# First batch by token halves, the inverse's updates on TensorE and ScalarE, and loads issued earlier, in a fused Nystrom attention and squared-ReLU kernel

## The chip, the cores and the metric

The kernel runs on one core of one Trainium2 chip. The metric is the device time of one execution in microseconds. The same program runs before and after on the same inputs.

## The reference

Eight batches of eight heads, 576 tokens, head size 64. The attention is approximated with 32 landmarks per head; the result goes through two GEMMs with a squared ReLU between them.

```python
B, H, S, D = q.shape                      # 8, 8, 576, 64
m = 32
q_lm = q.reshape(B, H, m, S // m, D).mean(axis=3)
k_lm = k.reshape(B, H, m, S // m, D).mean(axis=3)
A  = sm(q, k_lm)                          # softmax of a @ b.T / 8 over the last axis
Bm = sm(q_lm, k_lm)
C  = sm(q_lm, k)
Z = Bm.transpose(0, 1, 3, 2) / (norm1(Bm) * norminf(Bm) + 1e-06)
for _ in range(6):
    Z = 2 * Z - Z @ Bm @ Z
x = (A @ Z @ C @ v)                       # then heads side by side: 4608 x 512
h = x @ w_in                              # 512 -> 2048
r = np.maximum(h, 0.0)
out = (r * r) @ w_out                     # 2048 -> 512
```

## The kernel before

Each batch has three parts. `attention(b)` forms the landmark sums, the three softmaxes A, B and C, the inverse Z by six rounds, and `C @ v`; it then folds Z, `C @ v` and `w_in` together into a matrix G (256 x 2048, `g_mm`, L925 and L928), so that the first GEMM is A^T against G and x itself is never formed. `mlp_in(b)` has 16 steps f, one per 128 hidden columns: four matmuls of 288 tokens each (`in_mm`, L947) into two PSUM banks, a relu of all 576 tokens to bf16 (L964 on ScalarE, L966 on VectorE), and a square (L972 on ScalarE, L974 on VectorE or GpSimd). `mlp_out(b)` does the second GEMM by 128 tokens, 16 matmuls of 512 columns into one bank each (`o_mm`, L1019), evicts and stores; in batch 0 each tile is made in two runs of eight matmuls.

A is made in two parts, one per four heads (`a_mm` L872): transposed out of PSUM (`a_t` L883), its maximum (L887), the subtraction (L889), the exponential (L892), the sum, the reciprocal, the product (L900) and the transposition to A^T (`a_xp` L911). `in_mm` reads both parts, `("AT", z, 0)` and `("AT", z, 1)`.

In batch 0 the inverse is a chain. The state `st` holds P = Z B and Z side by side, 32 x 32 blocks of four heads on the partitions. A round is `nv_0` on TensorE (L688, eight matmuls of 32 x 32 blocks) and the update `upd` on VectorE (L703): the new state is 2 st minus the product. The sixth round gives `zt` (L713).

The loads go through GpSimd's queue: half of q or k of a batch (L372, 288 KB), a quarter of v (L377, 144 KB), a quarter of `w_in` (L404, 512 KB) or of `w_out` (L412, 512 KB). They are cast to bf16 on the way. Piece n of `w_in` is read by `g_mm` n, piece j of `w_out` by the `o_mm` of f = 4j to 4j + 3. GpSimd's other instructions stand in the same queue.

Nothing is scheduled at run time. `Plan.add` only records operations with what they read and write, and `Plan.emit` writes them out in the order of the list `ORDER`: each number holds an operation, its engine and its PSUM bank, and a negative one a run of dummy matmuls of zeros (`fill`, L453) that keep TensorE busy. Every engine then works through its own instructions in that order. A second table, `PACE`, adds waits: an operation in it does not begin before another operation is done, also where no data passes between them. Loads in particular are held back in this way: before, the first piece of `w_in` waits for `st0z`, the start of the inverse's state (L666).

Of the kernel before, what the change touches and what calls it, by code (L numbers as in the profile page):

```python
# [8 lines left out]
P = 128  # L9
# [22 lines left out]
SUMS = 2  # L32
LN_EXP_SET = 6
# [7 lines left out]
    592, 32, 344, 280, 72, 472, 720, -384, 2628, 2696, 2309, -56, 1606, 160, 200, 784, 408, 536, 1496, 1560, -56,  # L41
    1664, 1924, 1736, 1432, 2000, 2368, 1798, 1872, 2759, 2440, 2180, 2501, 2832, 3014, 3088, 2248, 3144, 3208, -16,
    6016, 6096, 2568, 2887, 2952, 1368, 2052, 920, 856, 984, 3280, 3344, 3408, 6160, 1048, 3472, 3536, 3600, 3664,
    2120, -34, 9733, 9800, 3728, 9158, 9216, 9288, 3780, 3920, 4992, 3856, 4738, 9349, 5072, 3972, 4048, 6598, 9416,
    5128, 4816, 5192, 1112, -37, 4100, 4176, -69, 4228, 4936, -13, 5381, 6232, 4872, -8, 5248, 6280, 6672, 4304, 5448,
    6736, 5520, 4356, 4432, 8454, 6352, 4487, 5320, 5632, 4560, 1176, 1240, 4615, 6416, 8900, 5584, 5712, 6808, 8512,
    1304, 4688, 5760, 6488, 5890, 6856, 6928, 6992, 6544, 7064, 9029, 9104, 9607, 8584, 8646, 5960, 5832, 7168, 7120,
    -42, 7362, 8968, 9680, 8712, 9860, 9936, 8773, 7960, 7304, 8024, 7240, -30, 15168, 15366, 8848, 8088, 18392,
    18328, 7440, 15440, 7496, 9992, 10056, 15240, 10128, 15304, 10192, 9476, 7554, 7696, 15552, 15750, 9552, 7624,
    8216, -13, 15938, 15504, 16132, 15624, 10256, 15816, 16008, 10384, 16320, 16514, 10448, 16710, 16200, 13252,  # L50
    15696, 10512, 16072, 15888, 16584, 656, 10328, 16400, -16, 7744, 10690, 16776, 7816, 13328, -19, 16902, 8152,
    17092, 10576, 10640, 10832, 18456, 10768, 16272, 10896, 7880, 16464, 16968, 13826, 17160, 16648, 17224, 8280,
    17280, 17352, 16840, 10950, 13904, 11024, 11088, -47, 12098, 20164, 13968, 11141, 18264, 8408, 22982, 11216,
    12176, 12232, 23040, 23104, 23168, 12296, 12352, 17032, 20224, 11280, 11333, 18759, 18816, 23232, 23296, 23360,
    13392, 25240, 12432, 18880, 18944, 19008, 19072, 23424, 11408, 12488, 11472, 14032, 11525, 24720, 12552, 11600,
    25296, 14088, 23496, 17474, 11664, 17544, 17664, 24784, 25360, 20288, 14160, 17736, 17800, 13464, 17416, 19136,
    12741, 12816, 12614, 14224, 12688, 8344, 20352, 12880, 20416, -10, 11717, 17856, 13512, 17608, 17928, 20480,
    11792, 11920, 21574, 21632, 21696, 11856, 11973, 25552, 12994, 20544, 12944, 25424, 24400, 12048, 24472, 19200,
    13072, 17992, 21760, 13125, 21824, 13192, 25624, 18048, 19272, 18120, 14786, 14920, 14856, 20608, 20680, 21888,
    21952, 14976, -53, 14402, 24536, 18648, 13584, -21, 14596, 22016, 18184, 26000, 24600, 13648, 25104, 22151, 22208,  # L60
    14296, 14352, 14480, 13720, 14536, 24856, 25688, 25752, 13776, 24920, 22272, 22336, 22400, 22464, 25496, 14664,
    24984, 14728, 25168, 22088, 22528, 24664, 31490, 31684, 25040, 25816, 23558, 23616, 15048, 22592, 18584, 25872,
    31560, 34648, 18520, 31752, 25936, 26050, 23680, 31876, 34776, 15112, 23744, 26128, 26192, 26312, 23808, 23872,
    22672, 23936, 22944, 26248, 26384, 24000, 26448, 26512, 26584, 28480, 28560, 28354, 31624, 28432, 34712, 19335,
    26640, 19392, 31944, 28624, 32008, 19456, 31816, 19520, 19584, 19648, 26948, 18712, 19712, 19776, 26704, 26768,
    26832, 20741, 20800, 26896, 27088, 27024, 20864, 20928, 20992, 21056, 21120, 19856, 20128, 20000, 28744, 28680,
    24080, 24224, 27160, 42136, 21184, 28808, 21264, 32066, 27204, 27280, 28872, 27344, 32256, 34584, 29200, 34904,
    30150, 30224, 20064, 19936, 32136, 29060, 32450, 32328, 32200, 27397, 27472, 27544, 32640, 30288, 29574, 29648,
    32520, 32712, 29128, 32408, 28933, 29000, 32834, 33024, 32912, 22880, 27588, 27664, 27728, 35078, 42640, 36423,
    36480, 33218, 27780, 21536, 33096, 42960, 43032, 32584, 27856, 27928, 35136, 33408, 29712, 32776, 36544, 29316,  # L70
    21472, 29784, 33488, 33288, 29264, 29392, 33602, 33792, 30360, 36608, 36672, 43344, 36736, 27972, 28048, 28112,
    32968, 33160, 33672, 28176, 33864, 29832, 33544, 35200, 35264, 42192, 42264, 42712, 33986, 42776, 42840, 29904,
    30408, 41816, 34176, 34248, 22816, 28228, 28304, 33352, 21408, 29968, 21344, 33736, 43096, 43160, 43224, 35328,
    35392, 36800, 36864, 36928, 35456, 35520, 29444, 29512, 34368, 34056, 34440, 34312, 36992, 30480, 42576, 37056,
    37120, 22752, 35584, 35648, 35712, 30544, 30616, 30914, 31048, 42512, 30720, 30792, 30992, 30864, 39108, 34504,
    34120, 39168, 42328, 30672, 33928, 39232, 37765, 37824, 35776, 39296, 31106, 31176, 31296, 31368, 31432, 37888,
    37952, 30040, 38016, 38080, 37184, 37248, 34968, 38144, 31248, 30096, 48898, 48968, 41872, 41936, 42896, 43280,
    42000, 35840, 35904, 24288, 35968, 42064, 39360, 45760, 42384, 42448, 43458, 43536, 43600, 43656, 43720, 24160,
    38208, 52184, 36032, 45840, 37312, 52440, 37376, 43792, 39424, 39488, 51992, 43856, 38272, 49032, 43920, 44048,
    37448, 45890, 45968, 44112, 46032, 46280, 46152, 39552, 39616, 37600, 38336, 38400, 46088, 39680, 44176, 44240,  # L80
    38464, 39744, 43408, 39808, 39872, 38528, 36112, 38592, 24352, 46216, 43992, 44359, 44496, 38656, 46608, 38720,
    38792, 39936, 44304, 40000, 52120, 49088, 46470, 49282, 49160, 37536, 40064, 52376, 40453, 49472, 46536, 35032,
    44432, 37664, 59024, 44568, 44614, 49360, 40512, 49666, 49224, 44688, 52056, 40576, 44752, 57872, 57936, 49544,
    49736, 40640, 44806, 36192, 46343, 46408, 46672, 44880, 44944, 47552, 46978, 47632, 40704, 44998, 45072, 34840,
    45144, 58008, 40768, 40832, 49800, 38944, 40136, 40896, 49856, 40960, 47696, 47768, 38880, 49608, 50054, 45188,
    47056, 47120, 49928, 41024, 41088, 50240, 58072, 49416, 45264, 45336, 50320, 37728, 50120, 50434, 53828, 50504,
    39072, 50000, 50192, 50568, 53888, 53952, 36256, 39008, 45382, 45456, 54016, 54080, 50384, 50624, 50818, 51014,
    45520, 40352, 47816, 45584, 58128, 50696, 51080, 54144, 47184, 58192, 58264, 58328, 47888, 47952, 54208, 54272,
    46720, 50888, 47240, 50760, 41152, 46800, 58712, 45638, 51202, 45712, 48024, 51392, 51472, 51272, 46854, 46920,
    50952, 36320, 36384, 52487, 54336, 52544, 47312, 51586, 51656, 48320, 48456, 48400, 47376, 52608, 41216, 59096,  # L90
    54400, 54464, 48130, 48208, 48512, 59160, 59224, 41280, 55174, 48656, 47448, 47504, 51336, 48264, 59288, 58776,
    55232, 58840, 58904, 48080, 48584, 55296, 58968, 58392, 58456, 51144, 48706, 48776, 52672, 52736, 51776, 48840,
    51856, 54528, 51928, 55360, 55424, 40416, 41344, 64962, 51528, 65152, 58512, 51720, 68184, 41408, 59344, 65032,
    65224, 52800, 41480, 52864, 59522, 58640, 41696, 59600, 59664, 59720, 59784, 52928, 58576, 59856, 68056, 59920,
    59984, 60048, 52992, 65344, 65416, 60112, 60176, 68120, 53056, 53120, 60240, 60304, 53184, 53248, 65538, 65728,
    65608, 52248, 60368, 60496, 55488, 55552, 53312, 60421, 60560, 60632, 54592, 54656, 54720, 54784, 65096, 65800,
    61954, 62032, 54856, 65480, 65288, 65864, 61824, 55616, 55680, 61904, 40288, 62096, 62344, 40224, 56516, 56576,
    56640, 56704, 60677, 60752, 55744, 55808, 68312, 68504, 62280, 62216, 62152, 41760, 41568, 55872, 65680, 60824,
# [172 lines left out]
def kernel(  # L271
# [152 lines left out]
    ident = sb.tile([P, P], BF16, name="ident")  # L424
    perm = sb.tile([P, P], BF16, name="perm")
    zero = sb.tile([P, P], BF16, name="zero")
    fold = sb.tile([P, 2, D], BF16, name="fold")

    def constants(e):
        make_identity(nc, ident[:])  # L430
# [656 lines left out]
```

## Time and profile before

| | us |
|---|---|
| median of 3 runs (lowest, highest) | 258.17 (257.74, 259.54) |
| profiled execution, its own time | 260.21 |
| its span, first to last instruction | 258.5 |
| TensorE busy, all matmuls | 245.5 |
| VectorE busy | 202.7 |
| ScalarE busy | 202.9 |
| GpSimd busy | 137.4 |
| second GEMM, L1019, 554 matmuls recorded | 138.5 |
| first GEMM, L947, 512 matmuls | 78.0 |
| dummy matmuls, L453, 109 | 11.5 |
| mean granted TensorE clock | 0.993 of full |

Busy times count each instruction from start to end, and those of one engine overlap a little, so a row's mean is longer than its share of the engine. A matmul's record includes the time until its result is out; back to back they follow each other faster. Idle time of an engine that nothing waits for costs nothing. The profile is of one execution, whose own time stands 2.0 us above the median of the three runs. DMA rates are those of the bytes that land.

### The profile page before, as it was taken

Reading aid. Unit: us, or ns where it says so; the run is one execution under the profiler, and the core shown is the slowest. Engines: PE = TensorE matmul, PEld = TensorE weight load, DVE = VectorE, ACT = ScalarE, POOL = GpSimd, SP = SyncE. Lnnn points to the kernel's source line nnn. Section 1 sums busy time; section 2 is a strip of 40 time slices with the busy share of each in tenths; the row PEclk is TensorE's granted clock in tenths of the full one; section 3 lists DMA queues with packets and bytes.
Section 4 is the critical chain, followed back from the end, with each engine's and each line's share of the span. In section 5 each row is a group of like instructions: output and inputs, shape, how many; then the busy total and the mean of one; then the engine's idle time right before and its main releaser. Section 6 shows DMA issues by size and latency. Waiting matters only on the chain.

```text
span 258.5 us, 7700 instructions
## 1 busy us (share of the span) xinstructions
PE 245.5 (95%) x2979; PEld 145.8 (56%) x3017; DVE 202.7 (78%) x495; ACT 202.9 (78%) x418; POOL 137.4 (53%) x211
## 2 busy tenths in 40 slices
PE   8996999989999999999999999999999999999994
PEld 8764665445654565555645465555645556466553
DVE  0497599989998998889989888887889887976210
ACT  3685699988997899988978799869889688647212
POOL 7369245877786556944676565745163362311500
PEclk9999799999999999999999999999999999999999
DMA  6999999839803990099405971088410252022114
GB/s 162 210 175 169 205 209 205 130 52 205 175 1 43 177 224 15 0 189 200 116 4 94 214 141 40 3 135 206 98 23 3 53 117 62 0 51 63 51 51 152
DMA packets 20467, 28.57 MB, mean 111 GB/s; under 512 B 3280, under 2 KB 11728, under 8 KB 20432
## 3 DMA queue, kind: packets, MB, share of 16 engines
q0 software_dynamic: 13296, 18.06, 43.9%
q1 hardware_dynamic: 6992, 9.90, 12.7%
q8 instruction: 23, 0.38, 0.6%
q10 hardware_dynamic: 144, 0.13, 0.2%
q14 instruction: 12, 0.10, 0.1%
HBM read 36.70 MB, written 9.44 MB: 178 GB/s over the span
## 4 chain that ended last, share of the span: by engine, by line
PE 78%; DMA 8%; DVE 5%; ACT 3%; issue 3%; POOL 1%; DVEq 0%; ACTq 0%; POOLq 0%
PE ps L1019 43%; PE ps L947 22%; DMA w_in_bf<-in_moe_w_in_dram 3%; DMA w_out_bf<-in_moe_w_out_dram 3%; PE ps L925 3%; PE ps L724 3%; DMA kraw<-in_k_dram 2%; PE ps L802 2%; PE ps L780 1%; PE ps L693 1%; PE ps L542 1%; PE ps L577 1%; POOL SA L889 1%; ACT r L964 1%; ACT EC L745 1%
## 5 line engine op out<-in xcount | busy, mean ns | idle before, releaser
L1019 PE MATMUL ps<-w_out_bf,gs 128*128 128x512 bf16 (+1 forms) x554 | 138.5, 373 | 3.5 <-issue 1.4
L1019 PEld LDWEIGHTS <-gs 128*128 128x128 bf16 x592 | 53.4, 98 | 48.2 <-issue 8.2
L947 PE MATMUL ps<-AT,G 128*128 128x288 bf16 x512 | 78.0, 288 | 0.1
L964 ACT ACTIVATE r<-ps 128x576 bf16<-128x576 f32 x104 | 65.0, 649 | 12.2 <-PE ps L947 9.8
L972 ACT ACTIVATE gs<-r 128x576 bf16<-128x576 bf16 x94 | 61.9, 684 | 2.6 <-DVE r L966 1.9
L947 PEld LDWEIGHTS <-G 128*128 128x128 bf16 x512 | 49.3, 99 | 23.9 <-issue 0.4
L974 POOL TENSOR_TENSOR gs<-r 128x576 bf16<-128x576 bf16 x16 | 18.3, 1146 | 27.0 <-DVE r L966 15.1
L303 ACT CAST G<-ps 128x512 bf16<-128x512 f32 x46 | 24.9, 597 | 6.8 <-PE ps L925 4.0
L377 POOL DMA_DIRECT2D vraw<-in_v_dram x32 | 18.2, 571 | 18.9 <-DVE Pd L635 6.2
L303 ACT COPY o<-ps 128x512 f32<-128x512 f32 (+1 forms) x29 | 16.4, 574 | 13.1 <-PE ps L1019 11.2
L966 DVE TENSOR_SCALAR r<-ps 128x576 bf16<-128x576 f32 x24 | 17.9, 751 | 7.1 <-PE ps L947 5.0
L900 POOL TENSOR_TENSOR EA<-EA,rA 128x576 bf16<-128x576 bf16 x16 | 18.4, 1159 | 6.5 <-DVE rA L898 4.7
L635 POOL TENSOR_TENSOR Pd<-st,ones_d 128x256 bf16<-128x256 bf16 x17 | 11.5, 677 | 11.9 <-DVE st L703 5.3
L745 ACT ACTIVATE EC<-ps,nmc 128x288 bf16<-128x288 f32 x24 | 11.7, 499 | 6.3 <-DVE nmc L738 3.5
L531 DVE STREAM_TRANSPOSE qT<-qraw 128x1152 bf16<-128x1152 bf16 x12 | 16.2, 1356 | 0.0
L531 DVE STREAM_TRANSPOSE kT<-kraw 128x1152 bf16<-128x1152 bf16 x12 | 16.2, 1346 | 0.0
L889 POOL TENSOR_TENSOR SA<-SA,mxA 128x576 f32<-128x576 f32 x10 | 11.6, 1164 | 6.4 <-DVE qs L510 2.9
L703 DVE SCALAR_TENSOR_TENSOR st<-st,ps 128x128 bf16<-128x128 bf16 x40 | 11.0, 276 | 3.0 <-PE ps L693 2.3
L305 DVE CAST G<-ps 128x512 bf16<-128x512 f32 x18 | 12.1, 681 | 1.2 <-PE ps L925 1.1
L453 PE MATMUL ps<-zero 128*128 128x128 bf16 x109 | 11.5, 259 | 1.4 <-DVE zero L462 1.1
L883 DVE STREAM_TRANSPOSE SA<-ps 128x576 f32<-128x576 f32 x16 | 12.1, 772 | 0.7 <-PE ps L872 0.3
L372 POOL DMA_DIRECT2D qraw<-in_q_dram x16 | 9.3, 583 | 5.6 <-DVE kT L305 2.8
(142 smaller groups left out, 355.6 us busy)
## 6 DMA issues: line engine op xcount, KB each, us to landing
out_dram<-o SPq DMA_DIRECT2D x126, 64.0 KB, 3.2
qraw<-in_q_dram POOLq DMA_DIRECT2D x16, 288.0 KB, 6.0
vraw<-in_v_dram POOLq DMA_DIRECT2D x32, 144.0 KB, 5.5
kraw<-in_k_dram POOLq DMA_DIRECT2D x15, 288.0 KB, 6.5
w_in_bf<-in_moe_w_in_dram POOLq DMA_DIRECT2D x4, 512.0 KB, 9.4
w_out_bf<-in_moe_w_out_dram POOLq DMA_DIRECT2D x4, 512.0 KB, 9.6
out_dram<-o SPq DMA_DIRECT2D x3, 256.0 KB, 2.0
gs<-in_k_dram SPq DMA_DIRECT2D x2, 288.0 KB, 4.1
```

Source lines behind the costliest of these rows:

```text
L303: nc.scalar.copy(dst, src)
L377: nc.gpsimd.dma_start(vraws[z][p0:p0 + 32, :, :, :].rearrange("p g t d -> p g (t d)"), src[b].rearrange(order, i=2, t=SEG)[i, :, :, c * NJ ...
L531: add("hx", "DVE", lambda e, nm=nm, raw=raw, i=i: nc.vector.transpose(heads(nm)[:, i, :, :, :].rearrange("p t h r -> p (t h r)"), raw[:, i ...
L745: add("c_exp4", "ACT", lambda e, sc=sc, i=i, c=c: nc.scalar.activation(EC[:, :, i, c, :], two(sc)[:, i, 0:HALF].rearrange("p (j r) -> p j ...
L889: keep("a_sub", add("a_sub", "DVE POOL", lambda e, part=part, spread=spread: ENG[e].tensor_tensor(part(SA), part(SA), spread(part(mxA)), A ...
L900: keep("a_mul", add("a_mul", "POOL DVE", lambda e, part=part, spread=spread: ENG[e].tensor_tensor(part(EA), part(EA), spread(part(rA)), AL ...
L947: mm(t[:, j, 0:HALF], lhsT=G[:, i, f * P:(f + 1) * P], rhs=AT[:, i, j * HALF:(j + 1) * HALF], start=(i == 0), stop=(i == 1))
L964: nc.scalar.activation(r.rearrange("p (j t) -> p j t", j=2), src, AF.Relu)
L966: nc.vector.tensor_scalar(out=r.rearrange("p (j t) -> p j t", j=2), in0=src, scalar1=0.0, scalar2=None, op0=ALU.max)
L972: nc.scalar.activation(dst, r[:], AF.Square)
L974: ENG[e].tensor_tensor(dst, r[:], r[:], ALU.mult)
L1019: mm(one(ok)[:, 0:hi - lo], lhsT=gs[:, f, x0:x0 + P], rhs=w_out_bf[:, f, lo:hi], start=(f == f0), stop=(f == f1 - 1))
```

## The change

It is made in batch 0 (`HALVES = 1`, `LESS = 1`), together with new lists `ORDER` and `PACE` for the whole program.

Tokens in two parts. `PARTS = ((0, 5), (5, 9))` cuts the 18 blocks of 32 tokens into 320 and 256 tokens of all eight heads. A is made by these parts rather than by heads, and `mlp_in(0)` does its matmul pair, relu and square for each part on its own.

```diff
+        for h, (lo, hi) in enumerate(PARTS if b < HALVES else ()):
+            n = hi - lo
+            sa, w, at = (A, "sa", h), 4 * n, 4 * lo
...
+                for i in range(2):
+                    for g in range(NG):
+                        for c in range(2):
+                            r = slice(64 * c, 64 * c + 64)
+                            mm(t[M * g:M * g + M, c, M * n * i:M * n * i + M * n], lhsT=dups["k"][r, i, g, :],
+                               rhs=Ts["q"][z][r, NJ * i + lo:NJ * i + hi, g, :], start=True, stop=True)
...
+            keep("a_xp", add("a_xp%d" % h, "DVE", a_xp2, reads=[("EN", z, h), ("EA", z, h)], writes=[("AT", z, h)]))
+        for i in () if b < HALVES else range(2):
...
+        for f in range(NF if b < HALVES else 0):
...
+            for h, (lo, hi) in enumerate(PARTS):
+                x0, x1 = 2 * M * lo, 2 * M * hi
+
+                def in_mm2(e, hk=hk, f=f, h=h, x0=x0, x1=x1):
+                    for i in range(2):
+                        mm(two(hk)[:, h, 0:x1 - x0], lhsT=G[:, i, f * P:(f + 1) * P],
+                           rhs=AT[:, i, x0:x1], start=(i == 0), stop=(i == 1))
+
+                op = add("in_mm%d" % h, "PE", in_mm2,
+                    reads=[("AT", z, h), ("G", z, f // 4, 0), ("G", z, f // 4, 1)] + ([hk] if h else []),
...
+                        nc.scalar.activation(r[:, x0:x1], src, AF.Relu)
...
+                        nc.scalar.activation(dst, r[:, x0:x1], AF.Square)
```

The inverse. A constant `two_i` holds -2 times the unit matrix in 32 x 32 blocks. Each round first adds -2 st into PSUM and then the product, so that an engine has only to copy the sum with its sign turned; ScalarE does it in all six rounds.

```diff
+                            if less:
+                                mm(t[r, i, lo:2, :], lhsT=two_i[r, :], rhs=st[r, i, lo:2, :],
+                                   start=True, stop=False)
                             mm(t[r, i, lo:2, :], lhsT=st[r, i, 0, :], rhs=st[r, i, lo:2, :],
-                               start=True, stop=True)
+                               start=not less, stop=True)
...
-            if it < 5:
+            if b < LESS and it < 5:
+                add("updn", "ACT DVE", lambda e, sn=sn, nv=nv: scaled(
+                    e, sn.rearrange("p i z m -> p (i z m)"), one(nv)[:, 0:4 * M], -1.0),
+                    reads=[nv], writes=[("st", (it + 1) % 2, 0), ("st", (it + 1) % 2, 1)])
```

The lists. Decoded, GpSimd's queue up to the last piece of `w_out` reads as follows (`tag.batch.turn`, and in brackets the operation that `PACE` makes it wait for; for v, `w_in`, `w_out` the turn is the piece, for q and k the half).

```
before: q.0.0 k.0.1 const1 q.0.1 const4 q.1.0 q.1.1 k.1.1 k.1.0 v.0.1 v.0.0 v.0.2 v.0.3[BB.0] w_in.0[st0z.0]
  a_sub.0.0[nmc.0.1] w_in.1[nmc.0.0] w_in.2[a_t.0.1] a_sub.0.1[a_max.0.1] w_in.3[upd.0.3] a_mul.0.0[rcv.0] a_mul.0.1
  w_out.0[a_xp.0.0] w_out.1[trev.1.2] v.1.0 q.2.0 k.2.1[trev.1.0] v.1.2[BB.1] mask.1.0 v.1.1 q.2.1[relu.0.6]
  v.1.3[square.0.6] k.2.0[mask.1.2] w_out.3[a_max.1.1] add9.2.2[mask.1.3] a_sub.1.0[add2.2.2] w_out.2[c_ev4.1]
after:  q.0.0 k.0.1 const1 q.0.1 q.1.1 k.1.0 const4 k.1.1 q.1.0 v.0.3 v.0.0 v.0.2 v.0.1 w_in.0 w_in.1[BB.0] w_in.2[st0z.0]
  w_out.1[nmc.0.1] v.1.2[a_max0.0] a_sub0.0[nmc.0.0] w_in.3[a_t1.0] a_sub1.0[rsum.0] a_mul0.0 a_mul1.0 v.1.0 w_out.0[a_rec.0.1]
  square0.0.0[mask.1.0] square0.0.1[cc.1] q.2.0[relu1.0.2] k.2.0[g_ev.0.5] k.2.1[relu1.0.3] q.2.1[square0.0.2]
  square1.0.5[mask.1.1] v.1.3 square1.0.7[a_t.1.0] v.1.1[a_t.1.1] w_out.2[relu1.0.9] w_out.3[square1.0.9]
```

On TensorE the changed order begins with 60 dummy matmuls (48 before), then a transposition of k and one of q before the sums. Its dummy matmuls are 106 in all (109). Before, `g_mm` 0, `g_mm` 1, B's scores of batch 1 and a transposition stand ahead of the first `in_mm`; now `g_mm` 0, a transposition and `g_mm` 1. ScalarE's queue from the inverse's start to its end is now:

```
updn c_exp1 c_exp0 updn c_exp0 c_exp1 updn l_ev.1 a_exp0 updn l_dup.1 l_dup.1 updn a_exp1 updn_0 trev.1 trev.1 Eb.1 Eb.1 g_ev
```

The evictions of the transposed C (`c_ev4`, `c_ev5`) and of WT go from ScalarE to VectorE in batch 0. Of batch 0's relus 21 parts are on ScalarE and 11 on VectorE, of its squares 24 on ScalarE, 4 on VectorE and 4 on GpSimd. For the later batches operations are listed in a new order and some change engines, such as three evictions of the second GEMM (ScalarE to VectorE).

## The prediction, made before the changed kernel ran

> **What bounds the kernel now.** I read the page's slices first, then the busy time in windows as long as one of the clock's periods, then the chain of work for the first 30 us, and last the same windows by batch.
>
> The slices of the page: TensorE is nearly full except at the start, where the granted clock also falls once.
>
> ```profile
> PE   8996999989999999999999999999999999999994
> PEclk9999799999999999999999999999999999999999
> ```
>
> The windows (columns: length, busy us of TensorE, its weight loads, VectorE, ScalarE, GpSimd, then clock, DMA share, GB/s):
>
> ```profile
> 15.90:19.31 3.41, 3.15 (x64) 2.26 (x56) 3.25 (x10) 3.28 (x12) 3.38 (x5) 1.00 1.03 150
> 19.31:22.73 3.42, 3.18 (x128) 2.57 (x125) 2.75 (x9) 2.17 (x6) 3.36 (x4) 1.00 0.96 134
> 22.73:26.14 3.41, 0.91 (x22) 0.61 (x25) 1.99 (x4) 1.70 (x4) 2.78 (x4) 1.00 1.24 205
> 26.14:29.55 3.41, 3.41 (x34) 2.46 (x34) 1.38 (x3) 1.84 (x7) 1.08 (x2) 0.50 1.24 205
> ...
> 50.03:53.44 3.41, 2.47 (x37) 1.34 (x31) 3.41 (x5) 3.41 (x8) 3.33 (x8) 1.00 0.46 74
> ```
>
> From 22.73 to 26.14 TensorE has 0.91 us of work, and in the next window it runs at clock 0.50. The DMA engines moved only 134 to 150 GB/s just before, against 205 to 209 later. The chain says why:
>
> ```profile
> 15.47 0.29 issue
> 15.76 0.43 POOL w_in_bf L404
> 16.19 0.35 issue
> 16.54 0.75 POOL SA L889
> 17.29 0.35 issue
> 17.65 8.38 DMA w_in_bf<-in_moe_w_in_dram
> 26.03 0.04 issue
> 26.07 0.58 PE ps L928 x2
> ```
>
> The second piece of w_in is issued at 17.65, behind a GpSimd subtraction and a wait, and lands at 26.03; all of TensorE's queue stands behind the product that needs it. The first GEMM (L947) starts at 27.61. Further on the whole chain has a second such stretch:
>
> ```profile
> 45.26 7.14 DMA w_out_bf<-in_moe_w_out_dram
> 52.44 1.67 PE ps L1019 x7
> ```
>
> By batch (first L947 of batch 0, 1, 2, 3 at 27.61, 53.95, 80.28, 107.10):
>
> ```profile
> 27.61:53.95 26.34, 24.86 (x312) 14.69 (x315) 24.90 (x64) 24.76 (x51) 15.32 (x27) 0.96 1.02 171
> 53.95:80.28 26.33, 26.01 (x332) 14.48 (x335) 24.87 (x59) 24.43 (x53) 19.63 (x30) 1.00 0.57 106
> 80.28:107.10 26.82, 26.24 (x334) 14.79 (x339) 23.73 (x65) 23.34 (x51) 16.60 (x28) 1.00 0.59 110
> ```
>
> In batch 0 VectorE and ScalarE are as full as TensorE, and part of TensorE's work there is dummy matmuls; from 54 us on TensorE is full with real work. So time can be won only before 54 us, and what is won there stays.
>
> **The change, part by part.**
>
> *Transfers.* The trace's landings on GpSimd's queue are in the order of issue: back to back a piece of w_in or w_out (512 KB) takes 2.5 us, half of q or k 1.4, a quarter of v 0.7. The last v of batch 0 lands at 18.36, but the first w_in, issued at 15.76, only at 23.49: 5.1 us for a 2.5 us piece. In the changed order it follows v without any wait, at about 9 us; the next two wait for steps reached at 13 and 15.5 us. So they go back to back behind v: w_in at 18.4 + 2.5 = 20.9, 23.4 and 25.9, then w_out's second piece 28.4, a v 29.2, w_in's last 31.7 (before 31.31), a v 32.4, w_out's first 34.9, four halves of q and k 40.5, two v 41.9, the last two of w_out 44.4 and 46.9 (before 47.80 and 52.40). On GpSimd two halves of a square stand ahead of batch 2's loads and two among the v; each takes some 0.65 and waits for its relu, so those issues come between 28 and 37, while the DMA queue still holds several us of work. The queue gets no deeper than it was at 25.02, when five w pieces and a v were under way and the issue took its usual 0.55 us.
>
> *Scores and inverse, batch 0.* TensorE now takes the transposes before k's sums: two of 0.34 us each, with an earlier q sum, so B's scores come at 11.5 instead of 11.01; VectorE puts one maximum less before the inverse, and its start comes at about 15.6 instead of 15.46. Then six rounds. Before, a round is eight small matmuls (0.24 us) and a VectorE update (0.28), and the last ends at 21.2. Now it is 16 matmuls and a ScalarE copy of 128x128. No row has that copy; the nearest are ScalarE's copies of 128x64 (0.22) and 128x128 (0.25), so 0.2 us start to start, bounds 0.1 and 0.28. What counts is the queue: between the first and the last update ScalarE has four exponentials of C with their sums (0.48 each), a sum's eviction (0.28), the two halves of A's exponential (0.63 and 0.52), two copies of 0.25 and six updates of 0.2: 5.05 us. From 16.3, the last ends near 21.4 to 21.6: 0.3 later than before, no gain. What VectorE gets back is 6 x 0.2 us in a window where it was busy 3.25 of 3.41.
>
> *To the first GEMM.* VectorE now evicts the transposed C and WT, behind A's sums: cv's product scaled at 21.7 (before 21.07), WT at 23.0 (22.38). g_mm of piece 0 at 23.1 (23.53), of piece 1 at 23.9 (26.07; its w_in is there at 23.4). A's first half needs maximum, subtraction, exponential, sum, product (GpSimd, 1.24 us) and transposes, ready at 23.8; G's two evictions now go to two engines, 24.4. First GEMM at 24.6: **-3.0 us**. Bounds: 23.9 if ScalarE's queue is 0.7 shorter; 27.0 if every step that I took start to start costs its whole duration.
>
> *Batch 0's stage.* Relu and square in parts of 320 and 256 columns. Whole, ScalarE needs 0.55 and 0.585 us start to start, VectorE 0.675 and 0.37. Of halves the nearest rows are C's exponentials of 320 and 256 columns, 0.53 and 0.47 long and 0.42 and 0.36 start to start: 0.23 more per pair. Two copies of 512 and 256 columns (0.48, 0.26) give only 0.05 more per pair. I take 0.06, by the copies, since relu has no bias or sum either: 1.1 us more on the two engines, and four square halves on GpSimd. Counting what the lists put between the first GEMM of batch 0 and of batch 1, with these durations: before 24.1 us on ScalarE and 25.6 on VectorE, now 23.1 and 23.5, because B's softmax of batch 1, two transposed copies and a q transpose stand elsewhere. 26.34 x 46.6 / 49.7 = 24.7: **-1.6 us**. With the exponentials' price for the pairs, 27 pairs x 0.17 = 4.6 us on two engines, or 2.3 us of time: +0.7. At the best -2.5, if the clock drop (1.7 us lost at 0.50) falls out on top. The last w_out piece at 46.9 lies below the first GEMM of batch 1 (24.6 + 24.7 = 49.3) and is needed just before it, with 2 us to spare.
>
> *After that.* What was moved out comes back: by the same count VectorE and ScalarE have 26.4 and 25.3 us before batch 2 (24.4 and 24.7 before), TensorE 0.4 more. TensorE-bound that is +0.4, by the ratio +1.4; I take **+0.6**. Then the counts of TensorE, loads and stores agree, and each load is issued 6 us or more of TensorE work ahead of its reader, as now: 0.
>
> Sum: -3.0 - 1.6 + 0.6 = -4.0. The profiled execution took 260.21 (span 258.5 and 1.7 around it); 256.2 for the like. The three times shown have their median 2.0 lower, 258.17, so **254.2**.
>
> *A rule against the row.* The granted clock halved after a window with 0.91 us of matmuls in 3.41, and stayed at 1.00 after one with 2.47. The changed order should have some 2.2 to 3.0 in each window between 16 and 26 us; if one falls too low, 1.7 us are lost. The Trainium skill, "TensorE: Matmul & The Clock Gate", Part 1, has the clock gated in free-running windows of 3413 ns and halved after an idle window. The trace agrees on the length, 3.41 us, but here the window before was not wholly idle; by the rule's letter only an empty window costs it, the sum stays, and the load-queue rival below would end at 259.3, within 1%.
>
> **The rivals.**
>
> *Work given back.* The head is won, but halves cost what the exponentials cost (+2.3) and batch 1's stage goes by the ratio (+0.8 over what I took): -0.9 is left, 257.3. For it: VectorE and ScalarE are full from 30 to 80 us. Against: relu and square stand closer to plain copies.
>
> *The load queue becomes the bound* (the slower side). Everything down to w_out's last piece is 8.9 MB in one order, and TensorE's list has a product waiting for it. At 205 GB/s it is there by 47; at the 171 GB/s of the row 27.61:53.95 only at 2 + 52.2 = 54.2. TensorE stands there at the place it now passes at about 53.0: 1.2 later, and a window that empties costs 1.7 at half clock: 261.0. It decides when that piece lands after about 53. For it: the lists put w_out and v ahead of w_in's last piece and q and k of batch 2 ahead of w_out. Against: the row's low rate comes from its end, when little was queued; while queued the windows have 205 to 209.
>
> *Transfers hidden anyway.* The first GEMM starts as late as now because the inverse's ScalarE queue, not w_in, ends last; then only the stage's -1.6 + 0.6 remain: 257.2. Against: WT at 22.38 was ready 3.6 us before w_in's second piece.
>
> *More than forecast.* Head 23.9, the stage's -2.5, nothing given back: -6.2, 252.0.
>
> **How the numbers follow.** One per cent, 2.6 us, is about what this measurement tells from no change. Forecast 0.60 (252.8 to 255.5), more than that 0.06, both faster by over 1%: 0.66. Work given back 0.16 and hidden 0.06, both within 1%: 0.22. Load queue 0.12, slower. Range 251.6 to 258.4: from a little past the largest gain to 1.1 past the smallest, leaving out the load queue and little else.
>
> **What would show it.** Right: the first L947 near 24.6; no clock of 0.50 between 22 and 30 us; no TensorE wait on w_in over 0.5 us; batch 1's first L947 at 48 to 50 and batch 2's at 75 to 77; TensorE's total the same. ScalarE's last update near 21.5. Wrong: first L947 past 27; a TensorE wait on w_out or v of several us between 40 and 55; ScalarE rows of half relus above 0.5 us; or a gap after 80 us that the profile of before lacks.

## The result and the profile after

The changed kernel takes **262.0 us** (median of 4 runs, 261.35 to 262.55) against 258.86 for the kernel before, measured beside it on the same chip: ratio **1.014 (95% interval 1.010 to 1.018)**, slower. The forecast was 254.2, range 251.6 to 258.4; it is wrong in sign and out of its range. The profiled execution took 261.76 us: span 259.7 and 2.0 outside it.

The page's slices. The thin slice of TensorE is the fourth as before, and thinner (5 for 6), and the clock falls in the fifth again:

```profile
PE   8995999999999999999999999999999999999995
PEclk9999799999999999999999999999999999999999
```

Windows as long as one clock period, laid on this run's own clock edges (columns as in the prediction: length, busy us of TensorE, weight loads, VectorE, ScalarE, GpSimd, then clock, DMA share, GB/s):

```profile
20.23:23.64 3.41, 2.96 (x136) 2.19 (x135) 3.19 (x11) 3.34 (x11) 2.86 (x3) 1.00 1.24 207
23.64:27.05 3.41, 0.67 (x13) 0.44 (x13) 0.39 (x2) 0.33 (x3) 1.58 (x3) 1.00 1.24 207
27.05:30.46 3.41, 3.41 (x25) 1.95 (x23) 2.33 (x10) 2.49 (x5) 0.71 (x1) 0.50 1.24 209
30.46:33.87 3.41, 3.41 (x35) 2.44 (x33) 3.28 (x11) 3.17 (x10) 2.34 (x4) 1.00 1.24 207
```

From 23.64 to 27.05 TensorE has 0.67 us of work, less than the 0.91 of before, and VectorE and ScalarE have next to nothing: everything waits for TensorE. The DMA engines run at full rate here (207 GB/s), as the forecast had it. The chain of work from 20 to 31 us says what TensorE waits for (columns: start, us, what; "issue" is time in which the engine waited for nothing that the profile shows):

```profile
22.47 0.25 DVE rA L916
22.72 0.08 DVE nmb L631
22.80 0.27 DVE WT L312 x2
23.07 0.04 issue
23.11 0.39 PE ps L998
23.50 2.88 issue
26.38 0.41 PE ps L998 x7
...
28.27 2.60 PE ps L1019 x12
```

WT is copied at 23.07 and `g_mm` 0 begins at 23.11, within 0.1 us of the forecast. Then TensorE stops for **2.88 us in the middle of one operation**, after the first of `g_mm` 0's eight matmuls. All eight read the same WT and the same piece of `w_in`, which landed at 21.10; no semaphore stands between them. The first GEMM (now L1019) starts at 28.06, against 27.61 before and 24.6 in the forecast. By batch (first GEMM of batch 0, 1 and 2 at 28.06, 53.94 and 80.77):

```profile
28.06:53.94 25.88, 25.34 (x315) 15.00 (x313) 24.48 (x68) 24.39 (x71) 15.53 (x25) 0.95 0.92 153
53.94:80.77 26.83, 26.68 (x343) 14.75 (x344) 25.97 (x61) 25.81 (x55) 19.45 (x33) 1.00 0.64 113
80.77:108.03 27.26, 26.83 (x338) 14.83 (x336) 24.12 (x66) 22.88 (x49) 16.12 (x27) 1.00 0.53 100
```

What could stop an engine that waits for no semaphore? One line of the page's DMA queues (packets, MB, share of 16 engines), which the prediction had not looked at:

```profile
q8 instruction: 24, 0.39, 0.6%
```

24 packets, each 16 KB in the trace's records. TensorE's list has 6156 rows (3078 weight loads and 3078 matmuls, one row each); 0.39 MB / 6156 is 64 bytes a row, so I read a packet as a block of 256 rows of TensorE's own program, brought by queue 8. An edge is the place in the list where one block ends and the next begins. The row at which TensorE stopped is number 957 of the list. A packet on queue 8 began at 24.16 and took 0.97 us; TensorE goes on at 26.38. **Theory 1:** TensorE ran out of instructions. The first `g_mm` begins at row 955 in place of 823; the 132 rows that the change adds ahead of it are 96 of the -2I matmuls, 32 of A's halves and 28 of batch 1's work moved ahead, less 24 of dummies. So a block's edge moves from behind the start of the first GEMM to a place ahead of it. **Rival:** `w_in`'s third piece landed at 26.34, 0.04 us before TensorE went on; the stop is a wait for it that the records don't show.

### The profile page after: what moved, and what is told of

Same layout as the page of the kernel before. It is cut to its first block, busy times and chain, and to the rows that moved or that the text cites. A ratio compares the mean times of both kernels' runs of the same rounds, so it can differ in the third digit from the quotient of the medians.

```text
span 259.7 us, 7900 instructions
## 1 busy us (share of the span) xinstructions
PE 250.1 (96%) x3078; PEld 146.4 (56%) x3078; DVE 209.3 (81%) x512; ACT 197.3 (76%) x431; POOL 141.6 (55%) x217
## 4 chain that ended last, share of the span: by engine, by line
PE 71%; DVE 10%; DMA 7%; POOL 6%; issue 4%; ACT 1%; POOLq 0%; DVEq 0%
PE ps L1129 39%; PE ps L1053 19%; DMA kraw<-in_k_dram 7%; PE ps L750 2%; PE ps L1019 2%; PE ps L995 2%; DVE kT L545 1%; PE ps L828 1%; PE ps L711 1%; PE ps L806 1%; POOL SA L909 1%; POOL EA L970 1%; DVE sA L966 1%; PE ps L998 1%; DVE G L312 1%
## 5 line engine op out<-in xcount | busy, mean ns | idle before, releaser
L1129 PE MATMUL ps<-w_out_bf,gs 128*128 128x512 bf16 (+1 forms) x592 | 145.4, 374 | 0.0
L1074 ACT ACTIVATE r<-ps 128x576 bf16<-128x576 f32 x92 | 58.1, 649 | 19.7 <-PE ps L1053 17.0
L1053 PE MATMUL ps<-AT,G 128*128 128x288 bf16 x448 | 67.8, 286 | 0.1
L1053 PEld LDWEIGHTS <-G 128*128 128x128 bf16 x448 | 42.6, 98 | 21.3 <-DVE G L312 0.6
L1082 ACT ACTIVATE gs<-r 128x576 bf16<-128x576 bf16 x73 | 48.7, 686 | 2.0 <-DVE r L1076 1.7
L1084 POOL TENSOR_TENSOR gs<-r 128x576 bf16<-128x576 bf16 x18 | 20.6, 1148 | 19.4 <-DVE gs L1084 9.9
L310 ACT CAST G<-ps 128x512 bf16<-128x512 f32 x46 | 24.8, 599 | 7.0 <-PE ps L998 3.5
L384 POOL DMA_DIRECT2D vraw<-in_v_dram x32 | 18.4, 579 | 17.3 <-DVE BB L643 5.3
L970 POOL TENSOR_TENSOR EA<-EA,rA 128x576 bf16<-128x576 bf16 x14 | 16.2, 1157 | 4.9 <-DVE rA L968 3.5
L312 DVE COPY o<-ps 128x512 f32<-128x512 f32 x11 | 7.4, 686 | 12.2 <-PE ps L1129 12.1
L1076 DVE TENSOR_SCALAR r<-ps 128x576 bf16<-128x576 f32 x20 | 14.9, 752 | 2.4 <-PE ps L1053 1.6
L711 PEld LDWEIGHTS <-Pd 128*128 128x128 bf16 x84 | 7.2, 97 | 8.0 <-DVE Pd L649 2.0
```

The lines of the kernel that those rows point to most:

```text
L310: nc.scalar.copy(dst, src)
L312: ENG[e].tensor_copy(dst, src)
L384: nc.gpsimd.dma_start(vraws[z][p0:p0 + 32, :, :, :].rearrange("p g t d -> p g (t d)"), src[b].rearrange(order, i=2, t=SEG)[i, :, :, c * NJ ...
L970: keep("a_mul", add("a_mul", "POOL DVE", lambda e, part=part, spread=spread: ENG[e].tensor_tensor(part(EA), part(EA), spread(part(rA)), AL ...
L1053: mm(t[:, j, 0:HALF], lhsT=G[:, i, f * P:(f + 1) * P], rhs=AT[:, i, j * HALF:(j + 1) * HALF], start=(i == 0), stop=(i == 1))
L1074: nc.scalar.activation(r.rearrange("p (j t) -> p j t", j=2), src, AF.Relu)
```

## The experiments

Times are medians; "before" ran beside each group and had a median of 258.5 to 258.8.

### Is it the third piece of w_in, or the row?

In **e1_swap** two issues change places on GpSimd's queue, nothing else.

```diff
- ... w_in.1[BB.0] w_in.2[st0z.0] w_out.1[nmc.0.1] v.1.2 ...
+ ... w_in.1[BB.0] w_out.1[nmc.0.1] w_in.2[st0z.0] v.1.2 ...
```

> The kernel after, with the transfers of w_in quarter 2 and w_out quarter 1 issued in each other's place on GpSimd's queue; nothing else is changed, so TensorE's program is the same row for row. Theory 1 (TensorE stops because the next 256-instruction block of its program has not come): the stop after the first matmul of the first g_mm stays where it is, begins at about 23.5 us and ends at 26.2 to 26.6, although w_in quarter 2 now lands at about 28.8. Theory 2 (the stop is a wait for w_in quarter 2, which landed 0.04 us before it ended): the stop ends where the quarter now lands, near 28.8. Either way g_mm 2 comes after 28.8; time 262 to 264 by theory 1, 264 to 266 by theory 2.

263.31 us (one run). The piece now lands at 29.2. TensorE's rows in the timeline of e1_swap (start, us, engine, line, operation, count, and in brackets the idle time before and what ended it):

```profile
24.18 0.39 PE L998 MATMUL ps<-w_in_bf,WT 64*32 64x512 bf16 x1 [0.39 <-DVE WT L312]
26.92 0.62 PE L998 MATMUL ps<-w_in_bf,WT 64*32 64x512 bf16 x7 [2.36 <-issue]
```

The stop is at the same row and ends 2.3 us before that landing. The rival is out.

In **e2_wide_fills** four dummy matmuls of 128 columns become one of 512.

```diff
     def fill(bank, n):
+        while n >= 4:
+            mm(ps[:, bank, :], lhsT=zero[:], rhs=zeros[:], start=True, stop=True)
+            n -= 4
         for _ in range(n):
```

> The kernel after, with every run of four fill matmuls of 128 columns made one matmul of 512 columns (the same TensorE time, a quarter of the instructions): 98 rows fewer ahead of the first g_mm (857 in place of 955). Theory 1: the block that was missing begins 98 rows later in the kernel's work, behind the first in_mm; no stop over 0.5 us, first in_mm at 24.6 to 25.0, no half clock after it, time 262.0 - 3.4 (the stop and its wake) - 1.2 (half of the 2.4 us of in_mm now at half clock) = 257.4, 256.5 to 259. Theory 2 (w_in quarter 2): the stop stays and ends at 26.4, time 261.5 to 262.5.

261.34 us, ratio 1.010 (1.006 to 1.015). The place of theory 1 held, its size did not. The stop left row 957, which is now reached at 31 us; but another came, after exactly half of the 72 matmuls of `C @ v`, and that is row 701, 256 rows earlier:

```profile
23.68 0.51 PE L834 MATMUL ps<-vraw,ECT 64*32 64x64 bf16 x36 [2.62 <-issue]
```

I had counted rows only up to one edge. The rows saved were dummies at the very start, so TensorE came to row 445 later (17.0 against 15.7 us). That fits a block being asked for when TensorE comes to the edge one block earlier: packet 21.27, TensorE on at 23.68. What counts then is not the number of rows but how many TensorE has to take in the 6 us that a block needs here.

### Rows alone: the same arithmetic in fewer instructions

In **e5_one_two_i** the -2I term is one matmul of 128 partitions per round and `i`, in place of four of 32.

```diff
+                        if less:
+                            mm(t[:, i, lo:2, :], lhsT=two_i[:], rhs=st[:, i, lo:2, :], start=True, stop=False)
                         for g in range(NG):
...
-                            if less:
-                                mm(t[r, i, lo:2, :], lhsT=two_i[r, :], rhs=st[r, i, lo:2, :],
-                                   start=True, stop=False)
```

> The kernel after, with the same -2I term of the inverse's updates brought in by one matmul over 128 partitions for each i in place of four over 32: the same arithmetic, copies and order, 72 TensorE rows fewer ahead of the first g_mm (883 in place of 955), all of them between 15.7 and 22 us. Theory 1 (instruction supply): the boundary at row 957 now lies 72 rows later in the work, behind the first in_mm, and its block has come by then; no stop over 0.7 us, first in_mm at 24.5 to 25.2, no half clock, time 257.4 (256.5 to 258.7). Rival (the copies by ScalarE or the summing itself cost what run e3_no_two_i gave back): first in_mm at 27.5 to 28.5 as in the kernel after, 261 to 262.5.

The constant for it becomes a 128 x 128 matrix. **257.95 us, ratio 0.996 (0.994 to 0.999)**: 72 rows are worth 4 us. Timeline of e5_one_two_i:

```profile
24.21 0.41 PE L996 MATMUL ps<-w_in_bf,WT 64*32 64x512 bf16 x8
24.56 0.51 PE L590 MATMUL ps<-perm,kraw 128*128 128x128 bf16 x6
25.00 0.41 PE L996 MATMUL ps<-w_in_bf,WT 64*32 64x512 bf16 x8
25.34 0.34 PE L464 MATMUL ps<-zero 128*128 128x128 bf16 x3
25.73 1.64 PE L1017 MATMUL ps<-AT,G 128*128 128x320 bf16 x12
27.53 0.23 PE L464 MATMUL ps<-zero 128*128 128x128 bf16 x1 [0.15 <-issue]
```

No stop in `g_mm`, no half clock between 20 and 250 us, and 0.15 us are left at row 957, now behind the start of the first GEMM, which comes 0.5 us later than the bounds I gave.

**e3_no_two_i** takes the -2I matmuls out altogether (VectorE's old updates, 2x - y, in the same places of the lists).

> The kernel after, with the inverse's updates done as in the kernel before (2x - y on VectorE, no matmuls by -2I): 96 rows fewer ahead of the first g_mm, spread over 18 to 22 us. Theory 1: no stop or one under 1 us before the first in_mm, which comes at 24.6 to 25.6; time 257.4 to 259.5. Theory 2: the stop still ends at 26.4; 261.5 to 262.5. If the shorter inverse is what the change lives on, the first g_mm comes 0.5 us or more later than 23.1.

258.37 us, ratio 1.001 (0.998 to 1.004). No stop; first GEMM at 25.43. `g_mm` 0 starts at 24.12 in place of 23.11: in these lists the inverse is shorter with the sums on TensorE (from its first `st` to `zt` 7.9 us here, 6.5 in the kernel after, 7.2 in e5). With few rows (e5) that is worth 0.4 us between the medians, 1.2 between the ratios, whose intervals touch.

### The parts alone, on the kernel before

**e4_early_only** is the kernel before with only the first `w_in` issues moved; the last v, ahead of them in the queue, loses its wait.

```diff
- v.0.3[BB.0] w_in.0[st0z.0] a_sub.0.0[nmc.0.1] w_in.1[nmc.0.0] w_in.2[a_t.0.1] a_sub.0.1
+ v.0.3 w_in.0 w_in.1[BB.0] w_in.2[st0z.0] a_sub.0.0[nmc.0.1] a_sub.0.1
```

> The kernel before, with only the first three w_in transfers issued as early as in the kernel after (quarter 0 without a wait, 1 behind BB, 2 behind the inverse's start, ahead of GpSimd's first subtraction). Theory 1 (rows decide): TensorE's program has 823 rows ahead of the first g_mm, so the boundary that stops the kernel after lies behind the first in_mm here; the 1.75 us wait on w_in goes, first in_mm at 25.5 to 26.2, no half clock, time 258.9 - 1.75 - 1.0 = 256.1, 255.3 to 257.5. Rival (the wait only gives room to another one, early transfers being paid for by v and w_out landing later): 258.2 to 259.5.

**256.70 us, ratio 0.992 (0.990 to 0.995)**: faster than both kernels. First GEMM at 25.31, batch 1's at 50.14; the waits on `w_in` and `w_out` are gone. It has a stop of its own, 112 rows into `C @ v`, at row 703, whose block is 1 us late:

```profile
19.67 0.62 PE L802 MATMUL ps<-vraw,ECT 64*32 64x64 bf16 x56 [0.24 <-ACT ECT L303]
21.31 0.25 PE L802 MATMUL ps<-vraw,ECT 64*32 64x64 bf16 x16 [1.02 <-issue]
```

This stop is not free. The inverse's sixth round stands behind `C @ v` in TensorE's list: from the last update to `zt` it is 2.35 us here and 1.19 in the kernel before. The chain of work of e4_early_only runs through the stop on to A's sums:

```profile
19.67 0.62 PE ps L802 x56
20.29 1.02 issue
21.31 0.34 PE ps L802 x16
...
21.73 0.29 DVE cvb L815
22.02 0.13 DVE zt L713
22.14 0.67 DVE sA L896
```

**e6_early_less4** and **e7_early_less1** add the inverse's sums and ScalarE's copies to e4, in four matmuls and in one.

> Run e4_early_only's kernel with the inverse's updates summed on TensorE in four matmuls of 32 partitions and copied by ScalarE, as in the kernel after: 96 rows more ahead of the first g_mm (919 in place of 823). Theory 1: the boundary at row 957 to 961 now falls behind g_mm 1, which TensorE reaches at about 24.3 us; the block is asked for at 20 to 21.3 us and comes 6 us later; a stop of 2 to 3 us and a half clock, time 256.7 + 2.5 + 1.0 - 0.7 (the shorter inverse) = 259.5, 258.3 to 261. Rival (rows cost nothing, a shorter inverse gains): 255.7 to 256.7.

> The same as e6_early_less4 with the -2I term in one matmul of 128 partitions: the same sums and copies, 72 rows fewer (847 ahead of the first g_mm). Theory 1: the boundary lies behind the first in_mm, no stop over 0.5 us there; first in_mm 24.6 to 25.3; time 255.7 to 256.8, 3 us under e6_early_less4. Rival (rows cost nothing): the same as e6_early_less4 within 0.5 us.

e6 takes 260.61 us, ratio 1.006 (1.003 to 1.009). The stop came where it was expected, at row 959 (703 + 256), after seven of `g_mm` 1's eight matmuls. Timeline of e6_early_less4:

```profile
25.03 0.41 PE L941 MATMUL ps<-w_in_bf,WT 64*32 64x512 bf16 x7
27.49 0.39 PE L941 MATMUL ps<-w_in_bf,WT 64*32 64x512 bf16 x1 [2.06 <-issue]
```

This execution kept its clock at 1.000; six of e6's ten runs have 0.993. e7 takes 258.61, ratio 0.998 (0.996 to 1.001), 2.0 under e6 and without a stop over 0.5 us: the rows' price once more, in part through the clock, since e6's four runs at 1.000 have a median of 259.5. But e7 missed its own number by 2 us: it is 1.9 slower than e4. Its inverse ends later (zt copied at 23.09, in e4 at 21.93). ScalarE's timeline in e7_early_less1 shows the copies (`st`) standing behind C's exponentials and A's:

```profile
18.14 0.28 ACT L309 ACTIVATE st<-ps 128x128 bf16<-128x128 f32 x1
18.32 0.47 ACT L779 ACTIVATE EC<-ps,nmc 128x256 bf16<-128x256 f32 x1
18.68 0.20 ACT L779 ACTIVATION_READ_ACCUMULATOR EC<-ps,nmc 128x1 f32 x1
18.77 0.53 ACT L779 ACTIVATE EC<-ps,nmc 128x320 bf16<-128x320 f32 x1
19.18 0.21 ACT L779 ACTIVATION_READ_ACCUMULATOR EC<-ps,nmc 128x1 f32 x1
19.27 0.69 ACT L903 ACTIVATE EA<-SA 128x576 bf16<-128x576 f32 x1
19.84 0.28 ACT L309 ACTIVATE st<-ps 128x128 bf16<-128x128 f32 x1
```

**e12_less1_vector** tries just that: e7 with the copies on VectorE.

```diff
-                add("updn", "ACT", lambda e, sn=sn, nv=nv: scaled(
+                add("updn", "DVE", lambda e, sn=sn, nv=nv: scaled(
```

> Run e7_early_less1's kernel with the copies of the inverse's updates (-1 times the sum) on VectorE in place of ScalarE: the sums on TensorE stay. e7 was 1.9 us slower than e4_early_only; its steps of the inverse took 1.46, 1.70, 1.05 and 1.04 us where e4's took 0.86, 0.90, 1.12 and 0.87. If ScalarE's queue is what held them (the copies stand behind its exponentials and evictions): first g_mm back at 23.6 to 23.9, time 256.5 to 257.1. If the summing on TensorE is: 258 to 259.

256.90 us, ratio 0.992 (0.989 to 0.995): ScalarE's queue was the cause. And it is no better than e4: in this order summing on TensorE gains nothing. VectorE's copy lasts as long (0.29 us) as the update it replaces (0.28).

**e11_halves_alone** cuts batch 0's in_mm, relu and square in e4 into the two parts, each part in the place of the whole.

> Run e4_early_only's kernel with batch 0's in_mm, relu and square cut at the change's token halves (320 and 256 columns), both halves of an operation in its old place in the order; A is not cut, so nothing can start earlier: the price of the halves alone. 16 relus and 16 squares become 32 each. From starts of neighbours in the traces a pair of halves takes 0.04 us longer than the whole on ScalarE, 0.02 to 0.06 on VectorE, 0.1 on GpSimd; as VectorE and ScalarE set this stage: 0.4 to 0.8 us more, stage 25.3 to 25.6, time 257.3, 256.9 to 257.8. Rival (the halves hide in waits): 256.4 to 256.9.

257.61 us, ratio 0.996 (0.994 to 0.999), 0.9 over e4. The stage from the first GEMM to batch 1's, first e4_early_only, then e11_halves_alone:

```profile
25.31:50.14 24.83, 24.49 (x315) 14.23 (x314) 24.52 (x66) 24.36 (x53) 15.73 (x26) 1.00 1.09 182
```

```profile
25.81:51.44 25.63, 24.31 (x312) 14.50 (x315) 25.27 (x73) 25.55 (x78) 16.27 (x28) 1.00 1.04 173
```

In e4 VectorE is busy 24.52 and ScalarE 24.36 of 24.83 us, so I take them for the bound here; TensorE's share is as high, but 19 of its matmuls are dummies, and the next two runs drop them. The halves add 1.94 us to the two together and 0.80 to the stage. Batch 1's stage and the later ones are e4's to 0.03 us.

**e8_halves_no_fill** and **e10_early_no_fill** drop the dummies of that stage, from e3 (33) and from e4 (19).

> Run e3_no_two_i's kernel (halves, early transfers, the old updates) without the 33 fill matmuls between batch 0's first in_mm and batch 1's, which take 2.75 us of TensorE there. If TensorE itself sets that stage's length (it is idle 0.6 us of 25.1): stage 22.5 to 23.5 us, time 255.6 to 256.8. If the evictions of the halves by ScalarE and VectorE set it and the fills only stand in their waits: waits of 2 to 3 us on relus and squares in the fills' place, stage 24.5 to 25.1, time 257.8 to 258.6. I hold the second for likelier, 2 to 1.

> Run e4_early_only's kernel without the 19 fill matmuls (1.7 us of TensorE) between batch 0's first in_mm and batch 1's. In that stage of e4_early_only VectorE is busy 24.52 and ScalarE 24.36 of 24.83 us, so they set it and the fills stand in their waits: stage 24.5 to 24.8, time 256.4 (255.9 to 256.8), 0.0 to 0.5 under it, as e8 gave 0.35 to e3. If TensorE set the stage: 255.0 to 255.4.

e8: 258.02, ratio 0.996 (0.994 to 0.999), stage 24.92 in place of 25.05. TensorE is busy 22.63 us of it (24.36 with the dummies); the rest went into waits of 0.2 to 0.4 us on ScalarE and VectorE. e10: 257.07, ratio 0.993 (0.991 to 0.996), 0.3 above the range I gave and no better than e4; stage 24.97. Without the dummies the stage is no shorter than 24.8 us in either, so TensorE's time is not what bounds it.

### Does the block wait among the loads?

**e9_quiet** issues `w_in` 1, 2, 3, `w_out` 1 and a v behind GpSimd's second subtraction.

> The kernel after, TensorE's program unchanged row for row, with w_in quarters 1, 2 and 3, w_out quarter 1 and one piece of v issued together behind GpSimd's second subtraction (about 21 us) and not at 12 to 19 us, so that the load queue runs dry at about 21.2 us. If the block of instructions at row 957 is late because its 16 KB wait among the loads: its packet starts by 21.8 us in place of 24.16, the stop at row 957 is gone or under 1 us, and waits on w_in (quarter 1 lands near 24.5) stand in its place; first in_mm 24.8 to 26.5; time 258 to 260.5, as all later loads come 2 us later. Rival (a block takes 6 to 7 us whatever the loads do): the stop at row 957 still ends past 26 us; 262 to 264.

261.02 us, ratio 1.007 (1.004 to 1.011). Timeline of e9_quiet:

```profile
23.18 0.39 PE L998 MATMUL ps<-w_in_bf,WT 64*32 64x512 bf16 x1
24.99 0.62 PE L998 MATMUL ps<-w_in_bf,WT 64*32 64x512 bf16 x7 [1.43 <-issue]
```

Half of what was expected: the packet began at 22.78 in place of 24.16, 1.0 us past the bound I gave, and the stop went from 2.88 to 1.43, not under 1. The first GEMM (27.59) is past the bound I gave, and the time lies between the two ranges. The stop is shorter with the loads held back, but running dry does not bring the block at once: TensorE came to row 701 at 20.4, and from 20.8 to 21.7 the DMA engines moved nothing, yet the packet did not begin (window of e9_quiet, the last two columns DMA share and GB/s):

```profile
20.80:21.70 0.90, 0.90 (x100) 0.82 (x94) 0.74 (x4) 0.71 (x2) 0.90 (x2) 1.00 0.00 0
```

In the kernel before, too, the engines moved only 68 GB/s from 20.8 to 22.0, and the packet asked for at 20.3 began at 25.16. Over all the traces, from TensorE's coming to an edge to the start of the packet it is 0.2 to 4.8 us in the first 45 us. Later, where the DMA engines stand nearly idle, it is at most 1.5, and often the packet begins before TensorE is there. So a block among loads tends to come later; what it waits for is not shown.

| kernel | TensorE stops before row | packet begins | goes on | stop |
|---|---|---|---|---|
| after | 957 | 24.16 | 26.38 | 2.88 |
| e1_swap | 957 | 24.54 | 26.92 | 2.36 |
| e9_quiet | 957 | 22.78 | 24.99 | 1.43 |
| e2_wide_fills | 701 | 21.27 | 23.68 | 2.62 |
| e4_early_only | 703 | 18.89 | 21.31 | 1.02 |
| e6_early_less4 | 959 | 25.18 | 27.49 | 2.06 |

Six stops, all at edges 256 rows apart (the two lists count two rows differently from the start), all ending 2.2 to 2.4 us after a packet's begin. Four more kernels with e4's list (e10, e11, e13, e14) stop at row 703 too, for 0.85 to 0.95 us. That theory 1 holds is shown by the places, by e1, and by e5 against the kernel after and e7 against e6, where the same term takes 72 rows fewer.

### What sets the first GEMM once the stop is gone

**e13_early_reordered** moves both chains that end there ahead in e4's queues; **e14_early_again** and **e15_before_again** run beside it.

> Run e4_early_only's kernel with four things moved in the queues and nothing else: the sum and reciprocal of A's second half ahead of the scaled product on VectorE, the product for WT and its copies ahead of batch 1's k transposes and sums, and g_mm 0 ahead of the last two transposes. If the two chains set the first GEMM: WT copied at 22.4 to 22.7 (was 23.07 to 23.30), second half of A done by 24.0 (was 25.23), first in_mm at 24.6 to 25.0 (was 25.31), time 256.2 (255.8 to 256.6). Rival (a wait that takes their place, most likely the missing instruction block at row 703 to 715, until 21.3 us): first in_mm at 25.1 to 25.5, time 256.5 to 257.2.

> Run e4_early_only's kernel once more, beside e13 on the same chip: 256.7, 256.3 to 257.1; first in_mm 25.2 to 25.9 as k's first half lands earlier or later.

> The kernel before, unchanged, for a second profile. The 1.75 us wait on w_in is there again. If the mean clock of the run is 0.998 or more (no half window), first in_mm to batch 1's first in_mm takes 25.0 to 25.5 us in place of 26.34 and the time is 257.5 to 258.3; with a half window (0.992 to 0.994) it is 258.8 to 260.2 as in the first profile.

e13: 258.36, ratio 0.998 (0.996 to 1.000), worse than e4 and not as either theory had it. WT was copied at 22.92 to 23.24, but `g_mm` 0's evictions still stood on ScalarE behind the copy of k's sums, whose matmul I had left behind two transposes; G's first copy is at 26.60. And TensorE, now with more waits, lost its clock:

```profile
19.89:23.30 3.41, 1.88 (x107) 1.55 (x107) 2.92 (x9) 1.39 (x4) 3.36 (x4) 1.00 1.24 204
23.30:26.71 3.41, 3.41 (x35) 2.57 (x32) 1.23 (x3) 1.45 (x4) 1.35 (x3) 0.50 1.24 207
```

So the run does not decide the question of the chains. e14: 257.30, ratio 0.994 (0.991 to 0.997), 0.2 above the range I gave: e4's gain holds, and no version is better. e15: 258.13 in 8 runs, with the 1.75 us wait on `w_in` again; its profiled execution, 260.65, had two half windows (clock periods granted 0.50) on end, mean clock 0.987, a case that I had not allowed for.

## Why the prediction was wrong, point by point

**The head, -3.0: measured +0.45.** The landings came as worked out (last v 18.53 for 18.4; `w_in` 21.10, 23.65 and 26.34 for 20.9, 23.4 and 25.9), the last update's copy ran from 21.62 to 21.83 (its end was forecast for 21.4 to 21.6), WT and `g_mm` 0 came to 0.1 us. The step that failed is from "g_mm of piece 0 at 23.1" to "of piece 1 at 23.9": 0.8 us were forecast, and it took 4.1 (23.11 to 27.21), 2.88 of them the stop at row 957. I priced each added matmul by its time on the engine (a round's eight more at next to nothing) and never by its row in the list. Taking out 72 of the 96 rows of that term gave back 4 us (e5). The bound of 27.0 did not cover the stop either; it was made of durations too. Without the stop (e5) the first GEMM is at 25.73, -1.9; k's first transposition began 0.8 us later in that run than in the kernel after (8.44 against 7.67), the rest is open, see e13.

**Batch 0's stage, -1.6: -0.46; -1.3 without the stop.** 25.88 us, with 2.4 us of first GEMM at clock 0.50. In e5 it is 25.05 (24.7 forecast). That the size is nearly right without the stop is in good part luck: e4, which moves nothing out of the stage and has no halves, has 24.83. It has neither the half window nor the 0.92 us wait on `w_out` that the kernel before has in this stage, and the ratio of engine loads passed over both; how much each is worth was not measured apart. The halves add 0.80 us to e4's stage (e11, 25.63), and e5, with the halves and the new lists, is 0.6 shorter than that; this is as near as the runs come to a price for the work moved out. The price of the halves, 1.1 us on two engines, was of the right kind and too small: 1.94 (e11); the rows of half relus stayed under 0.5 us (0.42 on ScalarE, 0.45 on VectorE).

**After that, +0.6: +1.24**, and +0.9 in e5. e11 has e4's later stages unchanged, so it is the new lists and not the halves. From batch 1's first GEMM on TensorE waits 0.87 us between matmuls in e3 and 0.11 in e4, and e3 has eight more matmuls of batch 1's `g_mm` there.

**From the profile to the median, -2.0.** Measured: +0.2, as the median of the kernel after lies 0.24 above its profiled execution. I took the 2.0 for a property of the run that any version would share. Of 105 runs of the kernel before, beside the experiments and in e15, 55 have a mean clock of 0.997 or more and a median of 258.19; 48 have about 0.993, one half window, and 259.26. The profiled execution was of the second kind, so 1.1 of the 2.0 goes with that window. A version that has it less often, or always, has no such 1.1 to take off. All four runs of the kernel after have 0.992 to 0.993; e3, e5, e7, e8 and e12, whose profiles show no wait on `w_in` and no stop over 0.6 us before the first GEMM, have it in 1 of 44 runs. Taking the wait on `w_in` away is not enough, though: e4's kernel still has it in 3 of 15 runs (e4 and e14). The other 0.9 of the 2.0 is not explained. Then 2.05 us of the kernel after lie outside the span, 1.71 before: +0.34, in every kernel of its lists but e1 (1.81) and e9 (1.72). Why was not settled.

Sum for the profiled executions: 261.76 - 256.2 = 5.6 = 3.45 (head) + 1.14 (stage) + 0.64 (later) + 0.34 (outside the span). For the medians 2.2 comes on top, from the -2.0: 262.0 - 254.2 = 7.8.

**The rule that was weighed.** The window rule of the Trainium skill ("TensorE: Matmul & The Clock Gate", Part 1), read by its letter, would have let the clock stand, as no window was empty. The row decided rightly: 0.67 us of work in 3.41 halved it.

**The rivals.** None was this one. The load queue did not bind: no wait on `w_out`, though its last piece landed at 49.53, 2.6 later than worked out. The only rival that gave a longer time gave it for the load queue; the time came out longer through the instruction queue, so that its chance of 0.12 fell on the right side was luck. The Trainium skill has the mechanism ("Runtime: NRT & Kernel Launch", Instruction fetch mechanics): instructions come through a FIFO in 16 KiB blocks of 256, fetched over the engine's own DMA queue while the block before is executed. The traces agree on block and queue. The page calls the cost of an edge "mostly hidden"; here TensorE stood still at one edge for 1.0 to 2.9 us in six kernels, and the measurement decides.

## What to carry to other kernels

Count an engine's instructions as well as their time. With small matmuls TensorE took 256 rows in 3 to 5 us here, and a block of 256 needed 5.6 to 6.7 us to come while loads ran. The sign of it is an idle time with "issue" in the profile, at a row that no dependency explains. One matmul over 128 partitions in place of four over 32, for the same sum, was worth 4 us here. And move loads first, alone: the smallest part of this change was its whole gain (0.992). The work rearranged around it gave half of that back even without the stop (e5, 0.996), and with the stop all of it and more (1.014).

## What the runs showed of the hardware that I had not expected

- At five of the six stops a block of TensorE's program took 5.6 to 6.7 us from the edge that asks for it to its first instruction, while loads ran at 201 to 206 GB/s; in e9, where they paused, 4.6. Rows saved early only delay the next request (e2).
- The clock halved after windows of 3.41 us with 0.67 (after), 0.91 (before), 1.88 (e13) and 2.29 us (e2) of TensorE work; an empty window is not needed. But it stayed at 1.00 after windows with 1.86 (e6), 2.26 (e4) and 2.47 (before), so the busy time of a window alone does not decide it, and no threshold follows. The windows of e6_early_less4:

```profile
23.57:26.99 3.42, 1.86 (x33) 1.07 (x31) 3.05 (x6) 2.36 (x7) 2.49 (x3) 1.00 1.25 208
26.99:30.40 3.41, 2.91 (x43) 2.13 (x44) 2.20 (x5) 2.46 (x8) 1.79 (x4) 1.00 1.16 161
```

- While the clock is low, a window with 1.91 us of work did not bring it back in e2_wide_fills, whose windows on its clock edges follow; the second low window comes after the 1.91:

```profile
18.77:22.18 3.41, 2.29 (x84) 1.55 (x81) 2.51 (x8) 2.89 (x10) 3.00 (x4) 1.00 1.24 207
22.18:25.59 3.41, 1.91 (x75) 1.53 (x76) 1.23 (x5) 1.08 (x3) 0.68 (x2) 0.50 1.25 206
25.59:29.01 3.42, 3.42 (x29) 1.40 (x28) 2.94 (x11) 2.90 (x8) 2.32 (x3) 0.50 1.23 206
```

- One kernel has runs 1.1 us apart by such a window. That it depends on which part of a window a wait falls in is likely, and was not tested.
